# Running the FFN1 and Bu matmuls as 64-row halves in two lanes of the TensorE array

## The chip, the cores and the metric

The kernel runs on one core of one Trainium2 chip. The metric is the device time of one execution in microseconds (us), lower is better; a figure for a kernel is the median of its executions. One execution of each kernel was also profiled. With one core there is no second die to compare with. The runs are told apart below by the granted TensorE clock that each lists; a run that was marked as slow (over 1.5% above the fastest of its kernel) is here one in which the clock stood at half for a while, and it is left out of the ratios.

## The reference

The input x has 2048 time steps of 448 features. Two branches work on it and a gate mixes them.

```python
g = sigmoid((x * gate_w).sum(-1, keepdims=True))
# branch A: a diagonal complex state space model
Bu = einsum("bld,pd->blp", x + 0j, B_bar)          # 448 -> 448 complex
for t in range(L): h = Lam_bar * h + Bu[:, t]      # a scan over 2048 steps
a = 2 * einsum("blp,dp->bld", hs, Cmat).real + x * Dskip
# branch B: an FFN
b = silu(x @ w1) @ w2                              # 448 -> 1792 -> 448
out = g * a + (1 - g) * b
```

All matmuls of x contract over 448 = 3 x 128 + 64 rows. That odd 64-row rest is what the change is about. FFN1 means `x @ w1`, FFN2 the matmul with `w2`, Bu the matmul with B, y the matmul with C.

## The kernel before

x is transposed into `XT` (even and odd time steps apart, 3 full blocks of 128 rows and one of 64). FFN1 is done in four quarters `c` of 512 time steps, 14 blocks `fb` of 128 columns each. A block's result takes one of the eight banks of PSUM, the memory that TensorE writes its results to. A counter hands the banks out in turn, and another engine must empty a bank (an "eviction") before the program uses it again. Three full blocks run on the whole array ("mains"); the 64-row rests of two blocks run at the same time in the lower and the upper half of the array, in two lanes ("rests"). Four blocks are grouped, and rests come alternately last and first, so that the array changes its mode only once per group of four. The cut below is abridged.

```python
def ffn1_mm(c, fbs):
    banks = [nxt() for _ in fbs]
    rf = half[0]                      # rests first?
    def mains():
        for fb, bank in zip(fbs, banks):
            for j in range(3):        # (in one operation)
                pe.matmul(ps[:, bank, :], W1E[:, j, fb*128:(fb+1)*128], XT[:, x0 + j, hs], ...)
    def rests():
        for i, (fb, bank) in enumerate(zip(fbs, banks)):
            p = slice(64, 128) if up else slice(0, 64)
            pe.matmul(ps[:, bank, :], W1E[p, 3, fb*128:(fb+1)*128], x, ...)
    for part in (rests, mains) if rf else (mains, rests): part()
    half[0] = not rf
    return list(zip(fbs, banks))

def ffn1(c, f0=0, before_last=None):
    for f in range(f0, NFB, 4):
        got = ffn1_mm(c, list(range(f, min(f + 4, NFB))))
        # ... cut ...
        while got:
            # ... one or two banks ...
            ffn1_act(c, fb, bank, n)  # silu on ScalarE, gives the bank(s) back
            yield fb
```

A tracker notes for each operation which buffers it reads and writes and puts the waits in. Each engine executes its operations strictly in the order in which this program emits them. That order is set by hand, by generators which are advanced a few steps at a time. `g2` are the sums of the gate (16 on ScalarE, in four portions of four), `t3` is one set of three sine tables, `f` is FFN1's second quarter:

```python
f = ffn1(1)
run(f, 2)
bu(0, 1); bu(3, 1)
# ... cut ...
for i, _ in enumerate(f):
    if i == 1:
        run(t3)
    run(g2, 1)
run(g2); run(s0, 1); run(g3)
for q in range(4):
    ffn2(0, q)
```

So ScalarE's order in this passage is silu(4,5), 4 sums, silu(6,7), table 3, 4 sums, silu(8,9), 4 sums, silu(10,11), 4 sums, silu(12,13). FFN2 of the first quarter then takes the banks that silu(6,7) and silu(8,9) give back.

## Time and profile before

The time before was 140.47 us (3 runs, 140.32 to 140.97). The page of the profiled execution says what bounds it. In its lines PE is TensorE, PEld its weight loads, ACT ScalarE, DVE VectorE, POOL GpSimd and SP SyncE; a q behind the name means that engine's sequencer, and `A <- B` that A waited for B. First the busy times by engine, then two rows in 40 equal slices of the span (a digit is the busy share in tenths), then the chain of waits that ended last, by engine and by line:

```profile
PE 135.5 (97%) x723; PEld 64.1 (46%) x723; DVE 122.7 (88%) x151; ACT 95.0 (68%) x157; POOL 32.0 (23%) x36
...
PE   7999999999999999999999999999999999999992
...
PEclk9999999999999999999999999999999999999999
...
PE 95%; DVE 1%; issue 1%; DVEq 0%
PE ps L696 31%; PE ps L333 23%; PE ps L909 14%; PE ps L734 13%; PE ps L363 5%; PE ps L346 4%; PE ps L746 3%; PE ps L404 2%; DVE TMPS L933 1%; PE ps L417 1%; DVE XT L422 0%; DVEq L1045 0%; PE ps L397 0%; DVE Q L240 0%; DVEq L141 0%
```

TensorE works without a break and is 95% of the chain (L696 is FFN2, L333 and L363 are FFN1's mains, L734 Bu's mains, L346 and L746 the rests, L909 is y). The list of what TensorE waited for (total us, times, longest) has two entries, both in the first ten us:

```profile
PE ps L404 <- DVE SG L241: 1.0, 1, 1.0
PE ps L363 <- DVE XT L422: 0.2, 1, 0.2
```

What there is to save is the mode changes. The timeline of TensorE in Bu's third stage shows two of them (start, us, instruction):

```profile
76.95 2.75 PE L734 MATMUL ps<-XT,BT 128*128 128x512 bf16 x12
79.63 1.04 PE L746 MATMUL ps<-XT,BT 64*128 64x512 bf16 x8
80.60 2.76 PE L734 MATMUL ps<-XT,BT 128*128 128x512 bf16 x12
83.20 2.75 PE L333 MATMUL ps<-XT,W1E 128*128 128x512 bf16 x12
```

Twelve matmuls without a change would be 12 x 0.216 = 2.59 us up to the next start. The first line, which ends in a change, has 2.68; the third, which begins behind one, has 2.60. The second line's eight lane matmuls are four steps, 0.86 us, and took 0.97. The single starts in the trace are 0.216 us apart inside a mode, 0.309 to 0.312 at a change, and 0.22 to 0.23 for the step after it: about 0.105 us a change. The Trainium skill, page "TensorEngine Tiling (Array Packing)", Key Properties, says that changing the tiling mode drains the array; it gives no price, and this is one.

The last view to keep in mind is ScalarE's silus in FFN1's second quarter, from its timeline (blocks 4,5 / 6,7 / 8,9 / 10,11 / 12,13 in this order):

```profile
32.89 1.02 ACT L373 ACTIVATE AT<-ps 128x1024 bf16<-128x1024 f32 x1
36.04 1.01 ACT L373 ACTIVATE AT<-ps 128x1024 bf16<-128x1024 f32 x1
42.65 1.00 ACT L373 ACTIVATE AT<-ps 128x1024 bf16<-128x1024 f32 x1
45.78 1.00 ACT L373 ACTIVATE AT<-ps 128x1024 bf16<-128x1024 f32 x1
49.17 1.01 ACT L373 ACTIVATE AT<-ps 128x1024 bf16<-128x1024 f32 x1
```

ScalarE has no gap between 31.0 and 50.4 us. FFN2 starts at 38.2 us and its third tile, which needs silu(8,9)'s bank, at 43.7, right behind the end of that silu (0.386 us after the matmul before it instead of 0.189, so it already waits for 0.2 us).

### The profile page before, as it was taken

The page shows a single profiled execution, that of the slowest core. Times are in us where ns is not written, and L with a number is a line of the kernel's source. Part 1 is how long each engine was busy: PE and PEld are TensorE (multiplying, and loading weights), DVE is VectorE, ACT ScalarE, POOL GpSimd, SP SyncE. Part 2 cuts the span into 40 slices and gives each one's busy share as a digit, 9 for nine tenths or more (in the row PEclk, how much of TensorE's full clock was granted, in tenths as well). Part 3 has the DMA queues.
Part 4 walks back from the last instruction along what each step waited for, and adds up shares of the span by engine and source line. Part 5 has one row for each costly group of instructions (what it writes and reads, how often), then busy time and mean ns, then how long its engine had stood idle before and what let it go on. Part 6 is the DMA issues. An engine that isn't in the chain of part 4 may idle for free.

```text
span 139.4 us, 1938 instructions
## 1 busy us (share of the span) xinstructions
PE 135.5 (97%) x723; PEld 64.1 (46%) x723; DVE 122.7 (88%) x151; ACT 95.0 (68%) x157; POOL 32.0 (23%) x36
## 2 busy tenths in 40 slices
PE   7999999999999999999999999999999999999992
PEld 7443334334354534343555443435555555555561
DVE  0258968899999999999999999999999999999563
ACT  0348999989999949995999283977313436879100
POOL 7103999990000000099940000000000000000000
PEclk9999999999999999999999999999999999999999
DMA  3999598899763100020200000000000000221124
GB/s 113 338 264 257 69 197 138 263 388 293 144 112 69 39 0 0 16 63 0 63 12 0 0 0 5 0 0 0 0 0 0 5 0 4 95 99 66 50 82 132
DMA packets 24319, 11.77 MB, mean 84 GB/s; under 512 B 16564, under 2 KB 23864, under 8 KB 24312
## 3 DMA queue, kind: packets, MB, share of 16 engines
q1 hardware_dynamic: 22724, 10.57, 30.9%
q10 hardware_dynamic: 1588, 1.11, 2.6%
q8 instruction: 5, 0.08, 0.2%
q14 instruction: 2, 0.02, 0.0%
HBM read 5.51 MB, written 1.84 MB: 53 GB/s over the span
## 4 chain that ended last, share of the span: by engine, by line
PE 95%; DVE 1%; issue 1%; DVEq 0%
PE ps L696 31%; PE ps L333 23%; PE ps L909 14%; PE ps L734 13%; PE ps L363 5%; PE ps L346 4%; PE ps L746 3%; PE ps L404 2%; DVE TMPS L933 1%; PE ps L417 1%; DVE XT L422 0%; DVEq L1045 0%; PE ps L397 0%; DVE Q L240 0%; DVEq L141 0%
## 5 line engine op out<-in xcount | busy, mean ns | idle before, releaser
L696 PE MATMUL ps<-W,AT 128*128 128x448 bf16 x224 | 43.0, 352 | 0.0
L333 PE MATMUL ps<-XT,W1E 128*128 128x512 bf16 x147 | 33.6, 380 | 0.0
L696 PEld LDWEIGHTS ps<-W,AT 128*128 128x128 bf16 x224 | 21.8, 98 | 20.9 <-ACT AT L373 0.5
L373 ACT ACTIVATE AT<-ps 128x1024 bf16<-128x1024 f32 (+1 forms) x33 | 27.3, 893 | 5.0 <-PE ps L346 4.7
L333 PEld LDWEIGHTS ps<-XT,W1E 128*128 128x128 bf16 x147 | 13.7, 98 | 18.9 <-issue 3.4
L734 PE MATMUL ps<-XT,BT 128*128 128x512 bf16 x72 | 16.6, 379 | 0.0
L709 ACT ACTIVATE BT<-ps,GT 128x448 bf16<-128x448 f32 x8 | 5.1, 633 | 13.1 <-PE ps L696 13.1
L599 POOL TENSOR_TENSOR P<-P 128x4 f32<-128x4 f32 x5 | 5.3, 1057 | 28.1 <-DVE P L606 27.8
L909 PE MATMUL ps<-CO,VE 128*128 128x448 bf16 (+1 forms) x63 | 11.6, 332 | 0.0
L909 PE MATMUL ps<-CO,HS 128*128 128x448 bf16 x56 | 11.6, 352 | 0.0
L804 DVE TENSOR_TENSOR_SCAN G<-P,Q 128x1024 f32<-128x1024 f32 (+1 forms) x6 | 11.3, 1918 | 0.0
L734 PEld LDWEIGHTS ps<-XT,BT 128*128 128x128 bf16 x72 | 6.8, 98 | 9.0 <-issue 1.3
L756 ACT ACTIVATE VE<-ps 128x1024 bf16<-128x1024 f32 (+1 forms) x8 | 7.3, 918 | 5.1 <-PE ps L746 5.0
L770 DVE SCALAR_TENSOR_TENSOR HS<-VE,P,G 128x512 bf16<-128x512 bf16 (+1 forms) x10 | 8.1, 856 | 0.2
L909 PEld LDWEIGHTS ps<-CO,VE 128*128 128x128 bf16 x63 | 6.1, 98 | 4.7
L909 PEld LDWEIGHTS ps<-CO,HS 128*128 128x128 bf16 x56 | 5.5, 98 | 5.1
L758 ACT ACTIVATE HS<-ps 128x1024 bf16<-128x1024 f32 (+1 forms) x8 | 7.3, 918 | 0.5 <-PE ps L734 0.5
L770 DVE SCALAR_TENSOR_TENSOR G<-VE,P,HS 128x1024 f32<-128x1024 bf16 (+1 forms) x5 | 7.5, 1494 | 0.1
L363 PE MATMUL ps<-XT,W1E 128*128 128x512 bf16 (+1 forms) x25 | 7.0, 420 | 0.2 <-DVE XT L422 0.2
L767 DVE TENSOR_TENSOR Q<-G,COS 128x2048 bf16<-128x2048 f32 (+1 forms) x4 | 7.0, 1756 | 0.1
L767 DVE TENSOR_TENSOR Q<-G,SIN 128x2048 bf16<-128x2048 f32 (+1 forms) x4 | 7.0, 1750 | 0.0
L346 PE MATMUL ps<-XT,W1E 64*128 64x512 bf16 x25 | 6.8, 379 | 0.0
(119 smaller groups left out, 198.5 us busy)
## 6 DMA issues: line engine op xcount, KB each, us to landing
W<-in_B_w_dram SPq DMA_DIRECT2D x1, 1568.0 KB, 12.1
XN<-in_A_x_dram SPq DMA_DIRECT2D x1, 896.0 KB, 7.7
out_dram<-OT SPq DMA_DIRECT2D x8, 112.0 KB, 1.7
out_dram<-TMPS SPq DMA_DIRECT2D x7, 112.0 KB, 1.7
W1E<-in_B_w_dram SPq DMA_DIRECT2D x3, 224.0 KB, 4.0
HS<-HS SPq DMA_DIRECT2D x4, 128.0 KB, 2.3
W1E<-in_B_w_dram SPq DMA_DIRECT2D x1, 384.0 KB, 5.1
XN<-in_A_x_dram SPq DMA_DIRECT2D x1, 384.0 KB, 5.9
```

What stands on the lines that cost most here:

```text
L333: ins = pe.matmul(ps[:, bank, :], W1E[:, j, fb * 128:(fb + 1) * 128], XT[:, x0 + j, hs], start=(j == 0 and not rf), stop=(j == 2 and rf))
L346: ins = pe.matmul(ps[:, bank, :], W1E[p, 3, fb * 128:(fb + 1) * 128], x, start=rf, stop=not rf)
L363: T.op("pe", lambda pe, fb=fb, bank=bank, j=j, p=p, x=x: pe.matmul(ps[:, bank, :], W1E[p, j, fb * 128:(fb + 1) * 128], x, start=(j == 0), ...
L373: T.op("act", lambda e: e.activation(a[:, fb:fb + n, :], ps[:, bank:bank + n, :], AF.Silu), reads=[f"ps{bank + i}" for i in range(n)], wri ...
L696: ins = pe.matmul(ps[:, bank, 0:D], a[:, fb, q * 128:(q + 1) * 128], W2[:, fb, :], start=(first and fb == 0), stop=(fb == NFB - 1), skip_g ...
L734: ins = pe.matmul(ps[:, bank, :], bt(slice(0, 128), j, m), XT[:, 4 * odd + j, hs], start=(j == 0 and not rf), stop=(j == 2 and rf))
L756: T.op("act", lambda e: e.activation(VE[:, m0:m0 + n, hs], ps[:, be[0]:be[0] + n, :], AF.Copy), reads=pe_, writes=[f"V{m}_{h}" for m in ms])
L758: T.op("act", lambda e: e.activation(HS[:, m0:m0 + n, 8 + h * 512:8 + (h + 1) * 512], ps[:, bo[0]:bo[0] + n, :], AF.Copy), reads=po_, writ ...
L767: T.op("dve", lambda e: e.tensor_tensor(o, a, b, op), reads=reads, writes=writes)
L770: T.op("dve", lambda e: e.scalar_tensor_tensor(o, a, s, b, ALU.mult, ALU.add), reads=reads, writes=writes)
L804: T.op("dve", lambda e, c=c, init=init: e.tensor_tensor_scan(G[:, c, w], rb, Q1[:, c, w], init, ALU.mult, ALU.add), reads=[f"Q1{c}", "rr", ...
L909: ins = pe.matmul(ps[:, bank, c], state(kt, odd, m), CO[:, m, c], start=False, stop=(m == YB[-1]), skip_group_check=True)
```

## The change

Its intent is to stay in lane mode through FFN1 and Bu, but for the full row blocks of FFN1's first six blocks, which stay on the whole array. Each pair of blocks (two FFN1 blocks, or the even and the odd half of Bu) is done in three operations: the lower rows of one block in the lower lane and the upper rows of the other in the upper lane (3 steps), the 64-row rests (1 step), and then the same with banks swapped, so that each block gets its other half (3 steps). That is seven steps for two blocks, as before. Two lanes are kept from writing one bank at the same time (the closing list names the page that asks for it), so the swap has to wait until the first half has landed. To cover this wait, the swapped part of a pair, and with it the operation that empties its banks, is emitted only after the next pair's first four steps.

```diff
+        waiting = []
+
+        def settle():
+            while waiting:
+                b, after = waiting.pop(0)
+                b()
+                after()
+
+        def pair(e, o, keys, rkeys, after):
+            opening.update((e[0], o[0]))
+            lanes(e, o, (0, 1, 2), keys)
+            lanes(e, o, (3,), rkeys)
+            c = T.count["pe"]
+            settle()
+
+            def swapped():
+                T.passed("pe", c)              # wait for its own semaphore
+                lanes(o, e, (0, 1, 2), keys)
+            waiting.append((swapped, after))
 ...
-        def ffn1(c, f0=0, before_last=None):
-            for f in range(f0, NFB, 4):
-                got = ffn1_mm(c, list(range(f, min(f + 4, NFB))))
 ...
-                    ffn1_act(c, fb, bank, n)
-                    yield fb
+        def ffn1(c, f0=0, ahead=None):
+            for fb in range(f0, NFB, 2):
+                ffn1_pair(c, fb)               # after = its ffn1_act
+                if ahead and fb == 8:
+                    ahead()
+                yield
```

Bu's two copies out of PSUM (`bu_out`) become an `after` likewise. Small parts: the column matmuls at the start run on the whole array (with `R` padded to 128 rows) and earlier, one small DVE operation is folded into another, and FFN1's first seven blocks become six. The loops of the hand-set order (`run(g2, 1)`, `run(t3)`, `run(t1)`) stay where they were.

More of the change, by code (lines that the diff above doesn't have):

```diff
@@ L25 @@
 NFA = 7
+NF1 = 6
 NWARM = 24
@@ L109, in op, with passed @@
             st.r = {}
+    def passed(self, eng, c):
+        if self.known[eng].get(eng, 0) < c:
+            self.known[eng][eng] = c
+            self.ops[eng].append(("wait", self.sem[eng], c))
     def group(self):
@@ L185, in gated_mix @@
         ID = sb("ID", [128, 128], BF16)
-        R = sb("R", [4, 512], BF16)
+        R = sb("R", [128, 512], BF16)
         PV = sb("PV", [128, 4, 4], F32)
@@ L240, in gated_mix @@
         T.op("dve", lambda e: e.memset(Q1[:, 0, 0:128], 0.0), writes=["Q10"])
+        T.op("dve", lambda e: e.memset(R[:, :], 0.0), writes=["R0", "R1", "R2", "R3", "Rd"])
         T.op("dve", lambda e: e.memset(SG[0:64, 0:1], -1.0), writes=["SGa"])
@@ L311, in gated_mix @@
         n_bank = [0]
-        half = [False]
         def nxt():
@@ L316, in nxt @@
             return BANKS[(n_bank[0] - 1) % len(BANKS)]
-        def ffn1_mm(c, fbs):
-            odd, h = c // 2, c % 2
-            hs = slice(h * 512, (h + 1) * 512)
-            x0 = 4 * odd
-            banks = [nxt() for _ in fbs]
-            xk = XO[h] + [f"XR{h}b"] if odd else XE[h] + [f"XR{h}a"]
-            rf = half[0]
-            def mains():
-                for fb, bank in zip(fbs, banks):
-                    def mm(pe, fb=fb, bank=bank):
-                        ins = None
-                        for j in range(3):
-                            ins = pe.matmul(ps[:, bank, :], W1E[:, j, fb * 128:(fb + 1) * 128],
-                                            XT[:, x0 + j, hs], start=(j == 0 and not rf), stop=(j == 2 and rf))
-                        return ins
-                    wk = ["W1Ej0", "W1Ej1", "W1Ej2"] if fb < NFA else ["W1Ed"] if fb < NFA + 4 else ["W1Ee"]
-                    T.op("pe", mm, reads=wk + (XO if odd else XE)[h][:3], writes=[f"ps{bank}"])
-            def rests():
-                def rest(pe):
-                    ins = None
-                    for i, (fb, bank) in enumerate(zip(fbs, banks)):
-                        up = (i % 2 == 1) != bool(odd)
-                        p = slice(64, 128) if up else slice(0, 64)
-                        x = XT[p, x0 + 3, hs] if up == bool(odd) else XR[p, hs]
-                        ins = pe.matmul(ps[:, bank, :], W1E[p, 3, fb * 128:(fb + 1) * 128], x,
-                                        start=rf, stop=not rf)
-                    return ins
-                T.op("pe", rest, reads=["W1Ea0", "W1Ea1", "W1Ez0", "W1Ez1"] + xk, writes=[f"ps{bank}" for bank in banks])
-            for part in (rests, mains) if rf else (mains, rests):
-                part()
-            half[0] = not rf
-            return list(zip(fbs, banks))
@@ new lines, in gated_mix, with xh, rem_keys @@
+        LO, UP = slice(0, 64), slice(64, 128)
+        def xh(odd, h, j, p):
+            b = XT if j < 3 or (p is UP) == bool(odd) else XR
+            return (XT[p, 4 * odd + j, h * 512:(h + 1) * 512] if b is XT else XR[p, h * 512:(h + 1) * 512])
+        def rem_keys(odd, h, p):
+            return (XO if odd else XE)[h][3:] if (p is UP) == bool(odd) else [f"XR{h}{'b' if odd else 'a'}"]
+        waiting = []
[4 more added lines that the diff above has]
+                after()
@@ new lines, in lanes, with mm @@
+        def lanes(lo, up, js, reads):
+            def mm(pe):
+                ins = None
+                for j in js:
+                    for p, (bank, odd, h, w) in ((LO, lo), (UP, up)):
+                        ins = pe.matmul(ps[:, bank, :], w(p, j), xh(odd, h, j, p), start=fresh[bank] and j == js[0],
+                                        stop=not fresh[bank] and j == 2)
+                return ins
+            fresh = {bank: bank in opening for bank in (lo[0], up[0])}
+            opening.difference_update(fresh)
+            T.op("pe", mm, reads=reads, writes=[f"ps{lo[0]}", f"ps{up[0]}"])
@@ new lines, in gated_mix, with wj @@
+        opening = set()
+        def pair(e, o, keys, rkeys, after):
[8 more added lines that the diff above has]
+            waiting.append((swapped, after))
+        def wj(fb):
+            return ["W1Ej0", "W1Ej1", "W1Ej2"] if fb < NFA else ["W1Ed"] if fb < NFA + 4 else ["W1Ee"]
@@ new lines, in w1, with rem_ffn1, ffn1_pair @@
+        def w1(fb):
+            return lambda p, j: W1E[p, j, fb * 128:(fb + 1) * 128]
+        def rem_ffn1(odd, h, fb):
+            return [f"W1Ea{fb // NFA}", f"W1Ez{(fb + 1) // NFA}", *rem_keys(odd, h, LO), *rem_keys(odd, h, UP)]
+        def ffn1_pair(c, fb):
+            odd, h = c // 2, c % 2
+            banks = [nxt(), nxt()]
+            pair(*[(banks[i], odd, h, w1(fb + i)) for i in range(2)],
+                 wj(fb) + wj(fb + 1) + (XO if odd else XE)[h][:3], rem_ffn1(odd, h, fb),
+                 lambda: ffn1_act(c, fb, banks[0], 2))
@@ L355, in ffn1_first @@
         def ffn1_first():
-            banks = [nxt() for _ in range(NFA)]
-            for j in range(4):
+            banks = [nxt() for _ in range(NF1)]
+            for j in range(3):
                 for fb, bank in enumerate(banks):
-                    up = j == 3 and fb % 2 == 1
-                    p = slice(64, 128) if up else slice(0, 128 if j < 3 else 64)
-                    x = XR[p, 0:512] if up else XT[p, j, 0:512]
-                    T.op("pe", lambda pe, fb=fb, bank=bank, j=j, p=p, x=x: pe.matmul(
-                        ps[:, bank, :], W1E[p, j, fb * 128:(fb + 1) * 128], x, start=(j == 0), stop=(j == 3)),
-                        reads=[f"W1Ej{j}" if j < 3 else "W1Ez0" if up else "W1Ea0", "XR0a" if up else f"XTe0{j}"],
-                        writes=[f"ps{bank}"])
-                    if (j, fb) in ((0, 6), (1, 1), (1, 3)):
-                        yield
@@ L369, in ffn1_first, with ffn1_rem, mm @@
-            yield list(enumerate(banks))
+                    T.op("pe", lambda pe, fb=fb, bank=bank, j=j: pe.matmul(
+                        ps[:, bank, :], W1E[:, j, fb * 128:(fb + 1) * 128], XT[:, j, 0:512],
+                        start=(j == 0), stop=False), reads=[f"W1Ej{j}", f"XTe0{j}"], writes=[f"ps{bank}"])
+                    if (j, fb) in ((0, 5), (1, 2)):
+                        yield
+            yield banks
+        def ffn1_rem(banks, fb):
+            def mm(pe):
+                ins = None
+                for i, p in enumerate((LO, UP)):
+                    ins = pe.matmul(ps[:, banks[fb + i], :], w1(fb + i)(p, 3), xh(0, 0, 3, p), start=False, stop=True)
+                return ins
+            T.op("pe", mm, reads=rem_ffn1(0, 0, fb), writes=[f"ps{banks[fb]}", f"ps{banks[fb + 1]}"])
+            ffn1_act(0, fb, banks[fb], 2)
@@ L374, in ffn1_act @@
                  reads=[f"ps{bank + i}" for i in range(n)], writes=[f"AT{c % 2}_{fb + i}" for i in range(n)])
-        def ffn1(c, f0=0, before_last=None):
-            for f in range(f0, NFB, 4):
-                got = ffn1_mm(c, list(range(f, min(f + 4, NFB))))
-                if before_last and f + 8 == NFB + 2:
-                    before_last()
-                while got:
-                    fb, bank = got.pop(0)
-                    n = 1
-                    if got and bank % 2 == 0:
-                        got.pop(0)
-                        n = 2
-                    ffn1_act(c, fb, bank, n)
-                    yield fb
+        def ffn1(c, f0=0, ahead=None):
[4 more added lines that the diff above has]
+                yield
         def rd():
@@ L396, in mm_cols @@
             for pt in range(4):
-                ins = pe.matmul(ps[:, 7, pt * 8:pt * 8 + 4], R[0:4, pt * 128:(pt + 1) * 128],
-                                ID[0:4, 0:4], start=True, stop=True)
+                ins = pe.matmul(ps[:, 7, pt * 8:pt * 8 + 4], R[:, pt * 128:(pt + 1) * 128],
+                                ID[:, 0:4], start=True, stop=True)
             return ins
@@ L429, in gated_mix @@
         rd()
-        next(first)
         T.op("pe", mm_cols, reads=["R0", "R1", "R2", "R3", "Rd", "ID"], writes=["ps7"])
-        next(first)
         T.op("dve", lambda e: e.tensor_copy(
@@ L435, in gated_mix @@
             reads=["ps7"], writes=["PV"])
+        next(first)
         def double(i):
@@ L468, in gated_mix @@
         pact("dt", LDT, AF.Exp, ["PV"])
-        ptt("ph", col("dt"), LIM, ALU.mult, ["dt", "PV"])
+        T.op("dve", lambda e: e.scalar_tensor_tensor(
+            col("phf"), LIM, 1.0 / TWO_PI, col("dt"), ALU.mult, ALU.mult), reads=["PV", "dt"], writes=["phf"])
         ptt("ar", col("dt"), LRE, ALU.mult, ["dt", "PV"])
@@ L478, in gated_mix @@
         T.op("act", lambda e: e.activation(JK[:, 0:1], HP[:, :], AF.Silu), reads=["HP"], writes=["JK0"])
-        pts("phf", col("ph"), 1.0 / TWO_PI, None, ALU.mult, ALU.bypass, ["ph"])
         pts("phr", col("phf"), MAGIC, -MAGIC, ALU.add, ALU.add, ["phf"])
@@ L689, in ffn2 @@
             first = c != 2
+            settle()
             bank = nxt()
-            half[0] = False
             def mm(pe):
@@ L719, in bu, with bu_out @@
             ms = [6] if pt == 3 else [2 * pt, 2 * pt + 1]
-            hs = slice(h * 512, (h + 1) * 512)
             n = len(ms)
-            if n == 2 and n_bank[0] % 2:
-                nxt()
             be = [nxt() for _ in ms]
             bo = [nxt() for _ in ms]
-            rf = half[0]
-            def mains():
-                for odd, banks in ((0, be), (1, bo)):
-                    for m, bank in zip(ms, banks):
-                        def mm(pe, m=m, bank=bank, odd=odd):
-                            ins = None
-                            for j in range(3):
-                                ins = pe.matmul(ps[:, bank, :], bt(slice(0, 128), j, m), XT[:, 4 * odd + j, hs],
-                                                start=(j == 0 and not rf), stop=(j == 2 and rf))
-                            return ins
-                        T.op("pe", mm, reads=(["BR"] if pt == 3 else BTK[0:2]) + (XO if odd else XE)[h][:3],
-                             writes=[f"ps{bank}"])
-            def rests():
-                def rest(pe):
-                    ins = None
-                    for m, b0, b1 in zip(ms, be, bo):
-                        for odd, bank in ((0, b0), (1, b1)):
-                            p = slice(64 * odd, 64 * odd + 64)
-                            ins = pe.matmul(ps[:, bank, :], bt(p, 3, m), XT[p, 4 * odd + 3, hs],
-                                            start=rf, stop=not rf)
-                    return ins
-                T.op("pe", rest, reads=(["BR"] if pt == 3 else BTK) + XO[h] + XE[h],
-                     writes=[f"ps{b}" for b in be + bo])
-            for part in (rests, mains) if rf else (mains, rests):
-                part()
-            half[0] = not rf
+            keys = (["BR"] if pt == 3 else BTK[0:2]) + XO[h][:3] + XE[h][:3]
+            rkeys = (["BR"] if pt == 3 else BTK) + XO[h] + XE[h]
+            for m, b0, b1 in zip(ms, be, bo):
+                pair(*[(b, odd, h, lambda p, j, m=m: bt(p, j, m)) for odd, b in ((0, b0), (1, b1))], keys, rkeys,
+                     (lambda: bu_out(pt, h, ms, be, bo)) if m == ms[-1] else (lambda: None))
+        def bu_out(pt, h, ms, be, bo):
+            hs, n = slice(h * 512, (h + 1) * 512), len(ms)
             m0 = ms[0]
@@ L956, in gated_mix @@
         s0, s3, s1, s2 = scan(0), scan3(), scan(1), scan(2, True)
-        for fb, bank in first:
-            ffn1_act(0, fb, bank)
-        run(ffn1(0, NFA))
+        ffn1_rem(first, 0)
+        ffn1_pair(0, NF1)
+        ffn1_rem(first, 2)
+        ffn1_rem(first, 4)
+        settle()
+        run(ffn1(0, NF1 + 2))
         run(t0, 2)
@@ L970, in gated_mix @@
         bu(3, 1)
+        settle()
         run(s0, 1)
@@ L983, in gated_mix @@
             run(g2, 1)
+        settle()
         run(g2)
@@ L1009, in gated_mix @@
         run(s2, 4)
-        run(ffn1(3, before_last=lambda: [ffn2_seed(q, 2 + q) for q in range(2)]))
+        run(ffn1(3, ahead=lambda: [ffn2_seed(q, 4 + q) for q in range(2)]))
         for q in range(4):
```

## The prediction

> **What bounds it now.** The chain that ended last is TensorE for 95% of the 139.4 us span; TensorE is 97% busy, and in the list of waits it waits only at the start (1.2 us together). In the trace, matmul starts are 216 ns apart for 512 columns (189 ns for 448). A pair of 64-row matmuls in two lanes also takes one 216 ns step, so nothing is won in steps: FFN1 and Bu need 294 before and after. Each change between whole array and lanes costs: start-to-start is 309-312 ns there instead of 216, and the next step 223-227; about 0.105 us. DVE has no gap from 24.9 to 129.1 us (timeline); ACT is gapless from 31.0 to 50.4.
>
> **What the change gives.** About two dozen mode changes become six: 18 x 0.105 = about 1.9 us. The small column matmuls come 0.7 us earlier, and one small DVE operation goes (0.2 us). Waiting for its own half bank should cost little: three or four steps (0.65 us or more) lie between, and a matmul takes 0.38 us.
>
> **What it takes.** The activation of an FFN1 pair is now put into ACT's stream one pair later, behind whatever was emitted meanwhile, and Bu's outputs likewise. In FFN1(1), ACT has the gate sums (4 take 2.23 us) and tables (3 take 3.2) between the activations. So silu(4,5) comes after four gate sums, silu(6,7) after the tables and eight sums, where silu(8,9) was. There are eight banks, and FFN2(0)'s first bank is the one that silu(6,7) frees. By the waits in the program, with durations from the trace:
> - Bu(0)'s second half waits for the last lane copy of Bu(3): about 2.4 us of TensorE wait near 24-27 us.
> - Pair (12,13) waits about 1 us for silu(4,5).
> - FFN1 would be done at 41 us, but silu(6,7) ends at about 45.3; FFN2(0) starts there (38.4 before): a wait of 4.4 us. Bu(1) then starts at 56 instead of 49.2: +6.8.
> - In the next stage table 1 stands ahead of Bu(1)'s second outputs, so a pair waits 1.8 us: net +1.1. The third stage gains 0.5.
>
> Together +7.4 us, all on the TensorE chain. DVE's last FFN2(0) eviction is 5 us later or more, which stays hidden behind TensorE (its slack was only about 0.5 us).
>
> **Clock.** The Trainium skill (TensorE: Matmul & The Clock Gate, Part 1) says the clock halves after an idle window of about 3.4 us in a free-running grid. This trace agrees: full clock at 6.57 us, half at 139.69, 3.2 us after the last matmul started, exactly 39 windows of 3.413 us apart. The 4.4 us wait can trip it: about 5.5 us of FFN2 at half clock, +2.8 us (estimate). I give that 60%.
>
> **Prediction.** 140.5 + 7.4 = 147.9, or 150.7 with the clock drop: 149.4 us, 145.0 to 152.5. Faster by over 2%: 0.02; within 2%: 0.06; slower: 0.92.
>
> **What would show it.** TensorE starts stay 216 ns apart in lanes. The list of waits shows TensorE waiting for ACT (several us, the largest before FFN2's first tile, around 41-45 us), then before Bu(0)'s second half and FFN1(2)'s third pair. The granted clock shows a 0.5 stretch near 44-51 us or none. The chain passes from TensorE to ACT between 20 and 45 us. DVE waits for TensorE at FFN2(0)'s evictions, some 5-7 us.
>
> **What would make it wrong.** ACT earlier than I summed (each us of ACT there is a us of the result); the first-half lateness being absorbed, in which case the result is 139-140, held by DVE's gapless stream; lanes slower than 216 ns in long streams, as weight loads of both lanes must hide in each step (10 ns per step would cost 2.8 us).

## The result, and the profile after

The changed kernel takes 152.26 us (4 runs, 151.11 to 153.28) against 140.72 for the kernel before in the same rounds; the ratio is 1.081, with a 95% interval of 1.0705 to 1.0917. A ratio here and below is the mean time of one kernel's runs over that of the other's runs of the same rounds, so it is not quite the ratio of the medians quoted. The output is correct, as it is for every kernel below. The runs lie in two groups by mean clock: 151.1 and 151.5 us at 0.989, 153.0 and 153.3 us at 0.976 to 0.977.

The same lines of the page of the profiled execution (a 151.51 us run at 0.989):

```profile
PE 135.0 (90%) x957; PEld 66.8 (45%) x957; DVE 122.8 (82%) x151; ACT 95.2 (64%) x152; POOL 31.1 (21%) x36
...
PE   7999696699616999996999999999999999999992
...
PEclk9999999999997899999999999999999999999999
...
PE 68%; ACT 16%; SPq 8%; DMA 3%; issue 1%; DVE 1%; ACTq 0%; DVEq 0%
```

TensorE's busy time did not grow; it has holes. The chain of waits now runs through ScalarE (ACT) for 16% of the span. The holes by name, from the list of what TensorE waited for:

```profile
PE ps L721 <- ACT AT L405: 4.3, 1, 4.3
PE ps L346 <- ACT VE L765: 2.3, 1, 2.3
PE ps L346 <- ACT VE L758: 1.6, 1, 1.6
PE ps L346 <- ACT AT L405: 1.5, 1, 1.5
PE ps L346 <- DMA XT<-in_A_x_dram: 1.2, 1, 1.2
```

L721 is FFN2, L346 all lane matmuls, L405 silu, L758 and L765 Bu's copies out of PSUM. The silus of FFN1's second quarter (4,5 / 6,7 / 8,9 and then 10,11 with 12,13 in one line) in ScalarE's timeline:

```profile
38.53 1.00 ACT L405 ACTIVATE AT<-ps 128x1024 bf16<-128x1024 f32 x1
45.12 1.00 ACT L405 ACTIVATE AT<-ps 128x1024 bf16<-128x1024 f32 x1
48.26 1.00 ACT L405 ACTIVATE AT<-ps 128x1024 bf16<-128x1024 f32 x1
51.65 1.92 ACT L405 ACTIVATE AT<-ps 128x1024 bf16<-128x1024 f32 x2
```

The second silu is 9.1 us later than before. Of this, 5.7 us come from the new order: it now stands behind silu(4,5), table 3 and eight sums instead of silu(4,5) and four sums. The other 3.4 us are the whole stream's lateness: ScalarE comes to this passage at 36.3 us instead of 32.9, after waits of TensorE further up (e5 comes back to this). FFN2 needs its bank and starts at 46.2 us instead of 38.2. The stretches by stage show the rest. The columns used here are: the stretch in us (set a little inside the stage), its length, the busy time of PE, PEld, DVE, ACT and POOL (with instruction counts), the granted clock, the DMA share and GB/s. For the changed kernel the rows are the hole ahead of FFN2's first quarter, that FFN2, Bu and FFN1 of the second stage, and Bu and FFN1 of the third:

```profile
41.50:46.10 4.60, 0.41 (x4) 0.00 (x0) 4.53 (x5) 4.54 (x13) 0.00 (x0) 1.00 0.34 77
46.20:58.50 12.30, 12.30 (x56) 5.87 (x56) 5.05 (x10) 7.53 (x22) 0.00 (x0) 0.86 0.01 1
58.60:77.10 18.50, 16.87 (x156) 7.31 (x155) 18.11 (x17) 12.42 (x13) 10.02 (x9) 1.00 0.12 29
87.90:104.60 16.70, 16.70 (x155) 7.39 (x153) 16.56 (x16) 11.08 (x13) 0.00 (x0) 1.00 0.01 2
```

The same three stages (without the hole, which it does not have) of the kernel before:

```profile
38.40:49.00 10.60, 10.57 (x56) 5.30 (x55) 10.53 (x12) 10.54 (x29) 0.00 (x0) 1.00 0.37 71
49.20:66.50 17.30, 17.30 (x89) 6.95 (x88) 16.95 (x20) 13.48 (x17) 6.87 (x6) 1.00 0.07 16
77.10:94.30 17.20, 17.20 (x90) 7.03 (x88) 17.09 (x17) 11.09 (x13) 0.00 (x0) 1.00 0.00 1
```

From the starts of the stages, the profiled loss up to the start of y is 125.7 - 115.4 = 10.3 us:

| part | before, us | after, us | difference |
|---|---|---|---|
| start of FFN2, first quarter | 38.2 | 46.2 | +8.0 |
| that FFN2 (clock 0.86 instead of 1.00) | 10.8 | 12.4 | +1.6 |
| Bu and FFN1, second stage | 17.3 | 18.5 | +1.2 |
| Bu and FFN1, third stage | 17.3 | 16.7 | -0.5 |
| the other FFN2s | 31.8 | 31.9 | +0.1 |

The third stage is the only one in which the change did what it was made for.

### The profile page after: what moved, and what is told of

It reads as the page before. It is cut to its first block, busy times and chain, and to the rows that moved or that the text cites. A ratio compares the mean times of both kernels' runs of the same rounds, so it can differ in the third digit from the quotient of the medians.

```text
span 149.8 us, 2402 instructions
## 1 busy us (share of the span) xinstructions
PE 135.0 (90%) x957; PEld 66.8 (45%) x957; DVE 122.8 (82%) x151; ACT 95.2 (64%) x152; POOL 31.1 (21%) x36
## 4 chain that ended last, share of the span: by engine, by line
PE 68%; ACT 16%; SPq 8%; DMA 3%; issue 1%; DVE 1%; ACTq 0%; DVEq 0%
PE ps L721 30%; PE ps L346 25%; PE ps L911 13%; SPq L231 6%; ACT VE L758 3%; DMA XT<-in_A_x_dram 3%; ACT CO L671 3%; ACT HS L760 2%; ACT COS L547 2%; SPq L228 2%; ACT VE L765 2%; ACT SIN L542 1%; ACT AT L405 1%; DVE TMPS L935 1%; ACT FP L545 1%
## 5 line engine op out<-in xcount | busy, mean ns | idle before, releaser
L721 PE MATMUL ps<-W,AT 128*128 128x448 bf16 x224 | 44.6, 362 | 4.3 <-ACT AT L405 4.3
L346 PE MATMUL ps<-XT,W1E 64*128 64x512 bf16 x325 | 40.0, 376 | 3.1 <-ACT VE L758 1.6
L721 PEld LDWEIGHTS ps<-W,AT 128*128 128x128 bf16 x224 | 22.2, 100 | 26.7 <-ACT AT L405 5.2
L405 ACT ACTIVATE AT<-ps 128x1024 bf16<-128x1024 f32 x28 | 27.9, 1017 | 4.8 <-PE ps L346 4.8
L346 PEld LDWEIGHTS ps<-XT,W1E 64*128 64x128 bf16 x325 | 17.4, 94 | 22.0 <-ACT VE L758 2.1
L346 PE MATMUL ps<-XT,BT 64*128 64x512 bf16 x168 | 20.0, 376 | 3.5 <-ACT VE L765 2.3
L758 ACT ACTIVATE VE<-ps 128x1024 bf16<-128x1024 f32 (+1 forms) x8 | 7.3, 915 | 17.3 <-PE ps L346 17.3
L346 PEld LDWEIGHTS ps<-XT,BT 64*128 64x128 bf16 x168 | 8.4, 94 | 13.9 <-issue 3.3
L346 PE MATMUL ps<-XR,W1E 64*128 64x512 bf16 x25 | 9.4, 376 | 0.0
L729 DVE SCALAR_TENSOR_TENSOR IOTA<-ps,GT,XN 128x448 bf16<-128x448 f32 x4 | 2.7, 684 | 7.3 <-PE ps L721 7.3
L935 DVE SCALAR_TENSOR_TENSOR OT<-ps,GT,BT 128x448 bf16<-128x448 f32 x4 | 2.7, 684 | 5.4 <-PE ps L911 5.4
## 6 DMA issues: line engine op xcount, KB each, us to landing
W<-in_B_w_dram SPq DMA_DIRECT2D x1, 1568.0 KB, 12.4
```

The costliest lines, as they stand in the source:

```text
L346: ins = pe.matmul(ps[:, bank, :], w(p, j), xh(odd, h, j, p), start=fresh[bank] and j == js[0], stop=not fresh[bank] and j == 2)
L405: T.op("act", lambda e: e.activation(a[:, fb:fb + n, :], ps[:, bank:bank + n, :], AF.Silu), reads=[f"ps{bank + i}" for i in range(n)], wri ...
L721: ins = pe.matmul(ps[:, bank, 0:D], a[:, fb, q * 128:(q + 1) * 128], W2[:, fb, :], start=(first and fb == 0), stop=(fb == NFB - 1), skip_g ...
L758: T.op("act", lambda e: e.activation(VE[:, m0:m0 + n, hs], ps[:, be[0]:be[0] + n, :], AF.Copy), reads=pe_, writes=[f"V{m}_{h}" for m in ms])
```

## The experiments

My theory was that the lanes are sound and that the loss comes from ScalarE's order: an eviction that is emitted one pair later lands behind whatever work the hand-set order puts between, TensorE runs out of the eight banks, and the holes also drop the clock. The rivals were that lanes, or a lane's wait for its own half bank, cost time themselves; that the eight banks are short whatever the order, because a pair stays open over the next one; and that the clock drop is harmless.

The runs in short; a time is a median, and the ratio is to the kernel before:

| run | time, us | ratio | 95% interval |
|---|---|---|---|
| changed kernel | 152.26 | 1.081 | 1.0705 to 1.0917 |
| e1_act_order | 147.93 | 1.043 | 1.0347 to 1.0519 |
| e2_before_late | 146.47 | 1.040 | 1.0341 to 1.0455 |
| e3_fill | 149.67 | 1.059 | 1.0532 to 1.0646 |
| e4_table1_spread | 150.37 | 1.063 | 1.0540 to 1.0713 |
| e5_bu3 | 149.66 | 1.063 | 1.0592 to 1.0661 |
| e6_combined | 139.56 | 0.993 | 0.9894 to 0.9957 |
| e7_whole_late | 149.25 | 1.061 | 1.0570 to 1.0646 |
| e8_swap_at_once | 148.09 | 1.053 | 1.0499 to 1.0557 |
| e9_combined_whole | 142.34 | 1.014 | 1.0102 to 1.0172 |
| e10_three_edits | 141.96 | 1.010 | 1.0071 to 1.0119 |

### e1: ScalarE's order as before, in the changed kernel

```diff
         for i, _ in enumerate(f):
-            if i == 1:
+            if i == 2:
                 run(t3)
-            run(g2, 1)
+            if i:
+                run(g2, 1)
```

> The changed kernel with one edit: in FFN1(1) the gate sums and table 3 are put into ACT's stream one iteration later, so that ACT has the order of the kernel before (silu(4,5), 4 sums, silu(6,7), table, 4 sums, silu(8,9), 4 sums, ...). Lanes, banks and swaps are as in the changed kernel. Theory (ACT's order): silu(6,7) ends at about 40.4 us instead of 46.1, so FFN2(0) starts at about 40.5 and at full clock; Bu(1) then waits for silu(12,13), whose end (53.6) does not move, and starts at about 53.7 instead of 58.6. Time 152.3 - 4.9 - (the part of the clock drop): 145.5 to 147.5 us. Rival (the lanes themselves, or waiting for their own half bank, cost the time): unchanged, 151 to 153 us.

It took 147.93 us, 0.4 us above the expected range; the four runs are one at full clock, 145.86 us, and three at 0.988, 147.9 to 148.3. So 4.3 us came back by the medians, and 3.3 us at equal clock (148.0 against 151.3 for the runs at 0.988 and 0.989), by moving work on an engine that is 64% busy. Of the 4.3 us entry 1.4 us are left, in two waits:

```profile
PE ps L346 <- ACT VE L765: 2.3, 1, 2.3
PE ps L346 <- ACT VE L758: 1.6, 1, 1.6
PE ps L721 <- ACT AT L405: 1.4, 2, 1.1
```

FFN2 started at 41.8 us and Bu's second stage at 55.0 (40.5 and 53.7 were expected). The surplus probably has a cause that I had not counted (the one run at full clock lies in the expected range): in the profiled run the clock had dropped earlier, from 27.9 to 31.4 us, around the 2.3 us wait of Bu's second half. The lanes were not touched, so the rival that blames them for all of the loss falls here.

### e2: the late order, in the kernel before

```diff
+        run(g2, 1)
         for i, _ in enumerate(f):
-            if i == 1:
+            if i == 0:
                 run(t3)
             run(g2, 1)
```

> The kernel before (whole array, no lanes, no late evictions) with one edit: in FFN1(1) ACT's gate sums and table are put one place earlier, so that ACT has the order of the changed kernel (4 sums, silu(4,5), table, 4 sums, silu(6,7), ...). Theory (ACT's order): silu(6,7) ends at about 42.8 us instead of 37.0, TensorE waits from 38.4 to 42.9 at FFN2(0)'s first tile, 145.0 us, up to 147 if the clock drops. Rival (the lanes): same as before, 140.5 to 141 us.

146.47 us, 5.5 us over the kernel before, with no lane and no late eviction in it. The list of what its TensorE waited for shows the one new entry:

```profile
PE ps L696 <- ACT AT L373: 4.4, 1, 4.4
PE ps L404 <- DVE SG L241: 1.0, 1, 1.0
PE ps L363 <- DVE XT L422: 0.2, 1, 0.2
```

It is the changed kernel's 4.3 us wait, at the same place (FFN2 starts at 42.1 us), made by order alone. The clock dropped in all four runs, so the time is in the upper half of what was expected.

### e3: the wait kept, the clock held up

```diff
+        T.op("pe", fill, reads=["ZW", "XTe00"], writes=["ps6", "ps7"])   # 19 matmuls of a zero tile, they add 0
```

The loop and the zero tile are cut. The matmuls stand between the last swapped part of FFN1's second quarter and its silu.

> The changed kernel, with 19 matmuls of a zero weight tile added into the last FFN1(1) bank (they add zero; 19 x 0.216 = 4.1 us) in the stretch in which TensorE waits for silu(6,7). The wait itself stays. Theory (the idle stretch drops the clock, which costs 1.8 us in one half of the runs and 3.5 in the other): granted clock 1.0 in all runs, FFN2(0) takes 10.6 us instead of 12.4, time 149.5 us and the runs within 0.5 us of each other. Rival (the clock drop is not on the path, or filling does not keep the clock): 151 to 153 us with the same spread.

Three of the four runs kept the clock at 1.0 throughout and took 148.98 to 150.15 us; the fourth, at 0.989, took 151.35. It is the profiled one: FFN2's first quarter took 10.7 us again, and the half clock lies from 27.2 to 30.6 us, in the earlier wait which the edit does not fill. So the drop is on the path and costs about 2 us (151.3 for the changed kernel's 0.989 runs against 149.4, the mean of the three; the changed kernel's profile has 1.6 us of it in FFN2), but it is a consequence of the waits: with the clock held, 8 to 9 us of the loss remain. The expected spread of 0.5 us was too narrow, it was 1.2 among the runs at full clock.

### e4: table 1 out of the way of Bu's second outputs

```diff
-        run(t1)
-        run(ffn1(2))
+        for i, _ in enumerate(ffn1(2)):
+            if 1 <= i <= 3:
+                run(t1, 1)
```

> The changed kernel, with table 1 (three ACT activations, 3.2 us) moved from ahead of Bu(1)'s second outputs to one each behind the silus of FFN1(2). Theory (an eviction behind other ACT work holds up TensorE): the 1.6 us wait of FFN1(2)'s third pair for VE goes, stage FFN1(2) lasts 16.8 us instead of 18.5, and as everything after is TensorE's chain the time falls by 1.6 to 1.7 us: 150.6. Rival (banks are short in any order because a pair stays open over the next one): the wait moves to another pair of the same stage, under 0.5 us gained.

150.37 us. The 1.6 us entry is gone from the list of waits and the second stage lasts 16.7 us instead of 18.5. At equal clock the gain is 1.6 to 2.0 us: 149.2 and 149.4 against 151.1 and 151.5 with one drop, 151.4 and 151.7 against 153.0 and 153.3 with two. The wait did not move to another pair, so eight banks are enough for the late swap when nothing stands before the evictions.

### e5: Bu(3)'s banks and the cosine of table 0

```diff
             be = [nxt() for _ in ms]
             bo = [nxt() for _ in ms]
+            if pt == 3:
+                be, bo = bo, be
 ...
         bu(3, 0)
-        run(t0)
         f = ffn1(1)
         run(f, 2)
+        run(t0)
```

> The changed kernel with two edits around Bu(3): its two banks change places, so that the bank that the lane copies read is not the one that Bu(0)'s second half opens first, and ACT's cosine of table 0 goes behind those copies. Theory: the 2.3 us wait of Bu(0)'s second half goes; as ACT, which paces this stage, was itself waiting for that half (2.0 us of ACT idle at 32 us), silu(6,7) and FFN2(0)'s first tile move from 46.2 to about 44.0, and the time falls by about 2.2 us to 149.0 to 151.0. The wait ahead of FFN2(0) stays at 4 to 5 us. Rival (ACT's own work alone sets silu(6,7)): FFN2(0) stays at 46, 151 to 153 us.

149.66 us, in the expected range, and FFN2 starts at 43.5 us (44.0 expected). The 2.3 us entry is gone; the 4.3 us one stays, and with it a clock drop in every run. The gain is somewhat larger than foreseen, 2.5 to 3.4 us at equal clock. The two edits were not tried apart, and this profile also lacks the wait for x (0.6 us for the copied B stands in its place), so part of it may be the chance of a DMA's landing. A wait of TensorE at 25 us had moved ScalarE's own stream, and through it a silu 20 us later.

### e6: all three, with a better order

```diff
         for i, _ in enumerate(f):
-            if i == 1:
-                run(t3)
-            run(g2, 1)
+            if i == 2:
+                run(g2, 1)
+                run(t3)
+            if i == 3:
+                run(g2, 1)
         settle()
         run(g2)                    # the other eight sums, after all silus
```

together with the edits of e4 and e5.

> The changed kernel with ACT's work in the order in which TensorE needs the banks: the edits of e4 and e5, and in FFN1(1) both silus (4,5) and (6,7) ahead of the first gate sums, then table 3, silu(8,9), the second gate sums, the last silus, and the other eight gate sums after them. Theory (the lanes are worth their mode changes once nobody waits for ACT): no TensorE wait over 0.7 us after 10 us but the one for the transposed x; FFN2(0) starts at 37.9 to 38.2, Bu(1) at about 48.6, clock 1.0, y about 1.7 us earlier than before; then DVE's stream, which ends only 0.6 us earlier, holds the last tiles: 139.0 to 140.0 us, ratio 0.988 to 0.995. Rival (lanes lose something by themselves): 141 us or more.

139.56 us (6 runs, 139.01 to 140.24), a little faster than the kernel before: ratio 0.993. The interval, 0.9894 to 0.9957, excludes 1, but the difference is far under the 2% from which the record calls a kernel faster (its word is "same"). The last of TensorE's listed waits (first) ends at 17.3 us, and the second and third stages (below, in the columns as above) last 16.8 and 16.7 us from Bu's first to FFN2's first matmul, against 17.3 before:

```profile
PE ps L429 <- DVE Q L246: 1.0, 1, 1.0
PE ps L346 <- DVE BT L594: 0.6, 1, 0.6
PE ps L387 <- DVE XT L447: 0.3, 1, 0.3
PE ps L422 <- DVE R L416: 0.2, 1, 0.2
```

```profile
48.10:64.80 16.70, 16.70 (x155) 7.23 (x151) 16.36 (x19) 14.37 (x25) 6.43 (x5) 1.00 0.07 17
75.60:92.20 16.60, 16.60 (x154) 7.30 (x151) 16.46 (x17) 10.98 (x13) 0.00 (x0) 1.00 0.01 2
```

One expectation did not come true: DVE did not hold up the last tiles. Its scan ended at 127.9 us instead of 129.1, and TensorE shows no wait for it. The profiled execution is 1.9 us shorter than that of the kernel before (137.5 and 139.4 us), more than the medians differ (1.1 us), since the clock happened to rise at 4.3 us in the one and at 6.6 in the other; the medians count.

### e7: the late order and the late evictions, on the whole array

```diff
-            lanes(e, o, (0, 1, 2), keys)
-            lanes(e, o, (3,), rkeys)
-            c = T.count["pe"]
+            for part in (rests, mains) if rf else (mains, rests):   # mains: 3 full blocks of each on the whole array
+                part()
             settle()
-            ...
-            waiting.append((swapped, after))
+            waiting.append((lambda: None, after))
```

> The changed kernel with its banks, its order of ACT and its late evictions, but the three full row blocks of each pair run on the whole array (only the 64-row rest in two lanes, alternately first and last, as before). No swap, no wait for its own half bank. Theory (order, not lanes): FFN2(0) starts at 45.5 to 46.5 as in the changed kernel, TensorE waits for the same ACT operations, and about one mode change a pair (0.105 us) makes stages two and three longer by 0.5 to 1 us each: 151.5 to 155 us. Rival (lanes): close to the kernel before, 141 to 143 us.

149.25 us: below the expected range, but over 6 us above what the rival wanted. I had expected all waits to stay. The 4.4 us wait for silu(6,7) did, but Bu's second half hardly waited (0.5 us), and FFN2 could start at 43.4 us:

```profile
PE ps L736 <- ACT AT L420: 4.4, 1, 4.4
PE ps L373 <- ACT VE L780: 0.5, 1, 0.5
```

Without lanes a block is complete earlier, and the wait for x is gone as well; ScalarE begins with Bu's copies at 20.6 us instead of 22.0. The share of each was not separated. Clock drops are in all four runs (0.975 to 0.988). The third stage lasts 17.7 us here. So a kernel without swaps loses 8.5 us. About 1.9 us of it is the price of its more frequent mode changes (e9 less the kernel before); the rest is order and late eviction, with the clock drops they bring.

### e8: no late eviction, the swap at once

```diff
-            c = T.count["pe"]
-            settle()
-
-            def swapped():
-                T.passed("pe", c)
-                lanes(o, e, (0, 1, 2), keys)
-            waiting.append((swapped, after))
+            T.passed("pe", T.count["pe"])
+            lanes(o, e, (0, 1, 2), keys)
+            after()
```

> The changed kernel without the delay: each pair waits for its own half bank, swaps and gives its bank to ACT at once, so ACT's order is that of the kernel before. Theory: no long ACT wait and no clock drop, but each of 39 pairs waits for its own last lane matmul (0.376 us long, 0.216 of it covered, plus the way of the semaphore): 0.25 to 0.35 us a pair, 10 to 13 us in all, so 148 to 152 us; the gaps are seen between the rest step and the swapped step. Rival (waiting for its own half bank costs nothing): 139 to 141 us.

148.09 us, at full clock in all runs (0.999 to 1.000), and without a ScalarE wait over 0.4 us. In the trace the step after the rests starts 0.441 us behind them instead of 0.216, and the step after that at 0.222. Stages two and three last 19.36 and 19.35 us. Against e6's 16.81 and 16.73 that is (2.55 + 2.62) / 22 pairs = 0.235 us a pair, a little under the expected 0.25. So the swap needs the next pair's work to hide its wait; the delay in the change was right, and what it delayed on ScalarE was overlooked.

### e9: e6's order, full blocks on the whole array

The edit is e7's in e6's kernel.

> The combined kernel (e6) with the full row blocks back on the whole array, as in e7: same order of ACT, same banks, one mode change for nearly every pair. Theory (what lanes are worth with nobody waiting for ACT is the mode changes alone): stages two and three last 17.7 us from Bu to FFN2 instead of 16.75, as e7's third stage did, and the first stage about 0.9 us longer too: 2.4 to 3.0 us over the combined kernel, 142.0 to 142.6 us. It is over the kernel before as well, which changes the mode once in four blocks. Rival (lanes are worth nothing, only the order of ACT was): 139.5 to 140 us.

142.34 us, as expected, at full clock and with no ScalarE wait in TensorE's list. Stages two and three last 17.8 and 17.7 us. With nobody waiting, lanes are worth 2.8 us by the medians against a mode change for nearly every pair (3.0 by the ratios; e6 and e9 ran in different rounds on different chips). Against the kernel before, which changed once in four blocks, e6's kernel wins 1.1 us as a whole, small parts included: stages two and three are 0.5 us shorter each. In the first stage, FFN2 starts 0.9 us earlier than before, but e6's clock rose 2.2 us earlier, which is worth about that much (estimate), and TensorE, early at Bu, waits 0.6 us there for the copied B. No run gave the better order to the kernel before; its TensorE was seen to wait for ScalarE for only 0.2 us (FFN2's third tile), so little can be won there.

### e10: e1, e4 and e5 together

> The changed kernel with the edits of e1 (ACT's order in FFN1(1) as in the kernel before), e4 and e5 together, without the better order of e6. Theory: FFN2(0) starts at about 38, but silu(8,9) and silu(12,13) stand behind gate sums as before, so the third FFN2(0) tile waits about 1.2 us and Bu(1) waits for silu(12,13), ending at 50.9 us as in e5; Bu(1) starts at 51.0 instead of 48.0, no wait is long enough to drop the clock: 142.0 to 143.2 us. Rival (the order of before is good enough for lanes too): 139.5 to 140.5 us.

141.96 us, a hair under the range, at full clock. Bu's second stage starts at 50.9 us (51.0 expected), and the entries are those foreseen, two waits of FFN2 (1.4 us together) and one of Bu (1.1), besides two for DMA of 0.5 and 0.2 us in the first 18 us:

```profile
PE ps L721 <- ACT AT L405: 1.4, 2, 1.1
PE ps L346 <- ACT AT L405: 1.1, 1, 1.1
```

The order that had just fitted the kernel before is not good enough for the changed one; e6's, with the sums that nobody needs soon at the end, is.

## Why the prediction was right

The prediction said 149.4 us, 145.0 to 152.5, slower with a chance of 0.92; the median measured is 152.26, only 0.24 us below the upper end. Two of the four runs, 153.0 and 153.3, lie above it, so that the median stayed inside is partly luck; slower, and why, was not.

- **TensorE starts stay 0.216 us apart in lanes: right.** The third stage, 77 steps, took 16.7 us, 0.217 each, with both lanes' weight loads hidden. The gain of 0.5 us that was foreseen for it was 0.5.
- **FFN2's first tile waits for silu(6,7): right.** 4.4 us foreseen, 4.3 measured; FFN2 started at 46.2 us (45.3 foreseen). e1 (order put back, 1.4 us of the wait left) and e2 (order alone moved, the same wait made in the old kernel) show the cause from both sides, and e7 shows it without lanes.
- **The other waits: right.** Bu's second half 2.4 foreseen and 2.3 measured, pair (12,13) 1 and 1.5, the pair behind table 1 1.8 and 1.6. e4 removed the third with about the gain foreseen (1.6 to 2.0 us for 1.6 to 1.7), e5 the first with a larger one (2.5 to 3.4 for 2.2).
- **The list that should show it: right.** The chain passes to ScalarE from 22 to 46 us, and DVE waits 7.3 us at the FFN2 evictions (5 to 7 foreseen). That loss stayed hidden behind TensorE.
- **The sum without the clock was too small.** It was +7.4; the profiled run shows 10.3 - 1.6 = 8.7. The term missed is the wait for the transposed x, 1.2 us in the list, which was not in the sum: the lanes reach Bu's rest earlier than the whole array did, and its DMA had not landed. Every profile of a kernel with late swaps has a wait at this place, but its length changes with the landing: 0.8 us in e1, 1.1 in e4, 0.2 in e10, and in e3, e5 and e6 0.6 us for the copied B instead. That it accounts for the difference was not tested by itself.
- **The clock was mis-sized.** It was put at 60% and 2.8 us. By the mean clocks it dropped in four of four runs, for one or two windows of 3.41 us each. The profiled run shows one, from 46.6 to 50.1 us, not the 5.5 us of FFN2 foreseen, and 1.6 us lost in FFN2 instead of 2.8. Between runs one window made about 2 us (e3), and two make the group at 153 us. Which waits made the second window in those two runs is open, as they were not profiled. In e4's profile, with the same waits but one, there are two separate stretches, at 27.9 and at 48.4 us; in e7's the two follow each other.

The Trainium skill, page "TensorE: Matmul & The Clock Gate", Part 1, carried this step: it describes a free-running window of 3.413 us. The trace agrees, with rises and falls a whole number of windows apart in each profile.

## What to carry to other kernels

When a change delays the emission of an operation, look at the engine on which that operation runs: on an engine that executes in order, "one pair later" means behind everything that was emitted in between, and an engine that is 64% busy can still hold up the array for 4 us. Count the PSUM banks from the end: which eviction gives back the bank that the next tile needs, and what stands in front of it. Work that nobody needs soon (here eight gate sums) belongs behind the evictions; with that order, and the edits of e4 and e5, the change was worth 0.7%, and without them it cost 8%.

## What the Trainium skill lacked or had wrong

- "TensorEngine Tiling (Array Packing)", Key Properties: that a change of mode drains the array agrees with the trace in that each change costs time, but it stands there without a price. Here it is about 0.105 us a change (0.309 to 0.312 us from start to start instead of 0.216, and about 0.01 in the next step).
- The same page, Gotcha 1 (row tiles must not use one bank at the same time, software must synchronise): no price of that is stated as such. A lane matmul that waits for TensorE's own semaphore starts 0.441 us after the last one instead of 0.216, 0.235 us lost a pair (e8); with three or more steps of other work between, nothing was lost (e6).
- No page says that two lanes can run a long stream at full rate with new weights in each step. They can: 0.217 us a step over 77 steps of two 64-row matmuls of 512 columns.
- "TensorE: Matmul & The Clock Gate", the table under "Why this matters for your kernels", allows idle gaps up to about 3 us. In e1's profile a gap of 2.7 us from start to start dropped the clock, as it lay in one window of the free-running grid (24.5 to 27.9 us), which had TensorE work for about 1.1 us; e3's and e4's profiles show the same. In the changed kernel's profile the same gap lay across two windows (they meet at 26.2 us) and dropped nothing.
- The same page, Part 1, has the clock halve after "≥1 idle window": the window need not be empty. In the changed kernel's profile the clock fell at 46.6 us, although FFN2 had begun at 46.2 in that window, and in e1's the window had 1.1 us of work.
